# A fused retention and mixture kernel: all TensorE products but the scores in the 128x64 split, decay every second chunk, one written order with written ring places

## The chip, the cores and the metric

The kernel runs on one core of a Trainium2 chip. The metric is the device time of one execution in microseconds (us). A core has five engines with queues of their own: TensorE (PE; its weight loads are listed as PEld), VectorE (DVE), ScalarE (ACT), GpSimd (POOL) and SyncE (SP), which here only issues DMAs. An engine takes its instructions in the order in which the program issues them. Matrix products are written to PSUM, a second on-chip memory, from which DVE or ACT must copy them.

## The reference

Inputs are q, k and v of shape 8 x 8 x 576 x 64 (batch, heads, tokens, head size), w_in (512 x 1024), w_out (1024 x 512) and g_ln (1024), all float32. First comes retention, attention with a fixed decay for each head in place of a softmax, then a two-layer block over 4608 tokens of width 512:

```python
scores = q @ k.transpose(0, 1, 3, 2) / 8
gamma = 1 - 2.0 ** (-5 - arange(8))
Dmat = where(rel >= 0, gamma[:, None, None] ** rel, 0)
attn = (scores * Dmat) @ v
x = attn.transpose(0, 2, 1, 3).reshape(4608, 512)
h = x @ w_in
solu = h * softmax(h)
ln = (solu - mean(solu)) / sqrt(var(solu) + 1e-6) * g_ln
out = ln @ w_out
```

Here rel is the query's position less the key's.

## The kernel before

**Chunks.** The 576 tokens of a batch element are cut into four chunks of 128 tokens (c = 0 to 3) and one of 64 (c = 4). The 64-token chunks of two elements are put together, so there are 36 chunks of 128 rows; n counts them, in groups of nine: two elements in turn for c = 0 to 3, then their common c = 4. Retention is computed chunk by chunk: inside a chunk as masked scores, and from the chunks before through a state (64 x 64 for each head) that is decayed and added to.

**Steps.** The work of a chunk is a set of small functions, the steps, each named by two letters and issued for a chunk by a token such as `tq:8` or `ex:5:a`, whose last letter names the engine (a ACT, v DVE, g POOL). In the order of the data:

- `ld` loads q, k and v (768 KB, SP queue). `cq`, `ck`, `cv` turn them into float16, q and v times a decay table (L205 to L224).
- `tq` transposes q and k on PE (L226), `eq` copies both out of PSUM. From chunk 12 on `kd` transposes k by DMA instead (L237), `tr` transposes only q on PE (L250) and `er` copies it. Chunks with c = 4 keep the first way.
- `sc` makes the scores: eight matmuls with 64 rows and 128 columns of weights, two at a time in the two row halves of the array (L283). `mk` masks them on DVE (L296).
- `kv` makes this chunk's addition to the state, eight matmuls with 64 columns of weights (L306). `ad` adds it to the decayed state, on DVE (L320; the sum is the tile t). `dk` makes from t the float16 state for the next chunk's query (L334), and `d3` the decayed float32 state for the next `ad` (L346), both on POOL. `d3` runs for c = 0 to 2.
- `av` multiplies the masked scores with v (eight matmuls with 64 columns of weights, L358); `fs` adds query times state to the same PSUM bank (L373; nothing for c = 0). `ex` copies the sum to xT.
- `m1` makes h in eight 512-column matmuls (L405; `mr` does the same in parts for the first two chunks, L393). `mx` takes the row maximum on DVE, `xp` exp on ACT, `so` the product u on DVE. In the first five chunks (PLAIN) `ce` subtracts the mean; for later chunks the mean is taken out of w_out once instead (`mm`, `mc`, `ws`).
- `sq` squares and sums on ACT; `rt` turns the sums into the row factor rs by three tiny POOL instructions (w, w, rs; L470). `tu` transposes u on PE in eight matmuls (lp, L491) and `eu` copies lp to uT; for seven late chunks `du` transposes u by DMA. `m2` makes the output in eight 512-column matmuls (L508), `st` scales it by rs and stores it.
- `li`, `lo` load the weights; `wi`, `wo` convert them. The last chunk is done in halves by steps that begin with h.

**Order.** Nothing is scheduled by a compiler: tokens are issued in written order, and so each engine's queue is filled. START (L26) is the written begin, LOOP (L43) a fixed pattern issued for 21 chunks, and END (L47) the written end. In LOOP the PE steps stand in the order tr, tu, m1, kv, av, sc, fs, m2.

**Places.** PSUM has eight banks of 2 KB for each partition. h takes two of two (tag h); the other four are given out by the digits in BANKS (L63), one for each tile in the order of issue. A tile that takes a bank waits until the reader of the tile before it in that bank is done. SBUF tiles rotate through rings of a fixed number of buffers (`bufs`).

**Shapes of the array.** A row of the profile such as `128*64 128x128` says that the weights have 128 rows and 64 columns, and that 128 columns are streamed. Before, `kv` and `av` are 128\*64 (each pair of matmuls fills the left and the right half of the array's columns), `sc` is 64\*128, and all others are 128\*128.

Of the kernel before, what the change touches and what calls it, by code (L numbers as in the profile page):

```python
# [13 lines left out]
P = 128  # L14
# [4 lines left out]


PLAIN = 5
FIRST = 7
STEP = 1
STOP = 28
BY_DMA = 12
START = """  # L26
ld:0 ld:1 c1:0 ck:0:g cq:0:v cv:0:v li:3 gt:0 c2:0 tq:0 cq:1:g cv:1:v ld:2 kv:0 ck:1:v tq:1 ad:0
eq:1:a d3:0 cq:2:v cv:2:g li:2 li:0 eq:0:a kv:1 wi:3:1:a sc:1 li:1 mk:1 dk:0 sc:0 ck:2:a ld:4
av:1 wi:3:0:a wi:2:1:g fs:1 tq:2 ld:3 mk:0 ad:1 av:0 ex:1:a wi:0:0:g eq:2:a fs:0 wi:1:1:a kv:2
mr:1:3 ad:2 d3:1 wi:1:0:g wi:2:0:v cq:4:g wi:0:1:v d3:2 sc:2 mr:1:0 ex:0:v ld:5 mr:1:2 ld:6  # L30
mr:1:1 mr:0:0 mr:0:2 mk:2 ck:4:g mx:1 xp:1 mr:0:1 mr:0:3 av:2 dk:1 mx:0 tq:4 eq:4:a so:1 cv:4:g
ce:1 wu:0:4 fs:2 lo:1 lo:2 cq:3:v sc:4 ex:2:a ck:3:g cv:3:g tu:1 xp:0 mk:4 m1:2 sq:1 tq:3 eu:1:a
dk:2 kv:4 eq:3:a ck:5:a kv:3 av:4 cq:5:g so:0 fs:4 ad:3 d3:3 sc:3 mx:2 dk:3 cq:6:g ex:4:a mk:3
ad:4 tq:5 cv:5:g xp:2 eq:5:a m1:4 lo:0 lo:3 sc:5 d3:4 so:2 cv:6:g mk:5 dk:4 kv:5 av:3 ck:6:a
fs:3 tq:6 d3:6 wo:4:g av:5 ex:3:a ld:7 eq:6:a wo:1:g mx:4 ad:5 wo:7:g kv:6 xp:4 m1:3 fs:5 ce:0
ce:2 wo:2:a ex:5:a tu:0 tu:2 sc:6 wo:5:a m1:5 ld:8 ad:6 so:4 wo:3:a eu:2:v mk:6 rt:1 wo:6:v
wo:0:a sq:0 d3:5 av:6 sq:2 mx:5 fs:6 ck:7:g mm:0 m2:1 cq:7:g ld:9 mx:3 eu:0:a rt:2 mc:0:v m2:0
ce:4 cq:8:v ws:3:v rt:0 xp:3 tu:4 ex:6:a ws:7:v ld:10 ws:4:v ck:8:g dk:5 st:1 xp:5 tq:7 sq:4
so:3 eu:4:v ld:11 eq:7:a m2:2 st:0 so:5 tq:8 ce:3 eq:8:a m1:6 ws:1:v ws:0:v cv:7:g sc:7 ws:2:g
tu:3 st:2 rt:4 ws:5:v ld:12 m2:4 mk:7 sc:8 sq:3 eu:3:a cq:9:g mx:6 mk:8 m2:3 st:4 dk:6 rt:3  # L40
cq:10:g kv:7 ck:9:a ws:6:v xp:6 cv:9:v ad:7 cv:8:v st:3 av:7 fs:7 ex:7:a ck:10:a ck:11:a
"""
LOOP = """  # L43
tr:2 so:-1 tu:-2 ld:6 er:2:v m1:0 dk:0 kv:1 eu:-2:a kd:4 ad:1 cv:3:g av:1 mx:0 sc:2 sq:-2 fs:1
ex:1:a rt:-2 cq:4:g xp:0 m2:-2 d3:0 ck:5:g st:-2 mk:2
"""
END = """  # L47
d3:-7 tr:-5 kd:-3 cq:-3:g kv:-6 av:-6 er:-5:v ld:-1 ad:-6 tr:-4 fs:-6 ex:-6:a dk:-7 sq:-9
so:-8 sc:-5 m1:-7 cv:-4:g er:-4:v mk:-5 tr:-3 kd:0 kv:-5 ck:-2:g av:-5 sq:-8 fs:-5 tu:-8 mx:-7
ad:-5 rt:-9 cv:-3:g dk:-5 er:-3:a tu:-9 kd:-2 m1:-6 xp:-7 sc:-4 kv:-4 cq:-2:v eu:-9:v so:-7  # L50
ex:-5:a m1:-5 sc:-3 mk:-4 rt:-8 du:-7 d3:-6 ld:0 mx:-6 eu:-8:a d3:-5 mk:-3 ad:-4 ck:-1:a dk:-6
m2:-9 av:-4 mx:-5 xp:-6 kv:-3 av:-3 d3:-4 cv:-1:g st:-9 d3:-1 ad:-3 kd:-1 cv:-2:g d3:-2 cq:0:g
fs:-4 fs:-3 so:-6 tr:-2 er:-2:v ex:-4:a xp:-5 m2:-8 sq:-6 dk:-4 sc:-2 mk:-2 ck:0:g m1:-4 so:-5
kv:-2 kv:-1 du:-5 ex:-3:a av:-2 sq:-7 st:-8 mx:-4 sq:-5 xp:-4 fs:-2 m1:-3 cq:-1:v cv:0:g kq:-1
rt:-5 dk:-3 ex:-2:a d3:-3 ad:-2 du:-6 tr:0 so:-4 er:0:a m2:-7 sc:0 m1:-2 ad:-1 mk:0 mx:-3
sc:-1 rt:-6 mk:-1 mx:-2 m2:-5 sq:-4 du:-4 kv:0 rt:-7 rt:-4 av:-1 av:0 fs:-1 dk:-1 m2:-6 st:-7
# [37 lines left out]
def kernel(  # L94
# [683 lines left out]
```

## Time and profile before

| | |
|---|---|
| median of 3 runs | 219.55 us (218.33 to 220.63) |
| the profiled execution | 218.18 us, its span 216.5 us (first to last instruction) |
| PE | 197.4 us busy (91%), 1989 matmuls; 1989 weight loads |
| DVE | 180.8 us (84%), 289 instructions |
| ACT | 167.1 us (77%), 279 |
| POOL | 173.6 us (80%), 275 |
| DMA | 47.04 MB, mean 217 GB/s |
| granted TensorE clock | 1.00 |

Busy time is the union of an engine's records. Matmuls are pipelined: a row "0.61 ... x8" is the time from the first start to the last end, and the next row may start before that end, so the pace is read from differences of starts. In a waits view a line says which engine's instruction, by line number, waited for which other, and then the total in us, the number of waits and the longest. "issue" is time in which the engine waited for nothing that the profile shows.

### The profile page before, as it was taken

How to read it: one execution, taken by the hardware profiler on the slowest of the kernel's cores; microseconds unless marked ns; L12 is line 12 of the kernel's file. 1: busy time of each engine (PE TensorE's matmuls, PEld its weight loads, DVE VectorE, ACT ScalarE, POOL GpSimd, SP SyncE). 2: the span in 40 equal slices, each digit the busy share in tenths (PEclk: the TensorE clock that was granted, in tenths of full speed). 3: DMA queues.
4: the chain of work that ended last, by engine and by line, in shares of the span. 5: the costliest groups of instructions: out<-in, count | busy, mean ns of one | idle time of the engine just before them, and what ended most of it. 6: DMA issues, size and time to landing. Idle time of an engine off the chain costs nothing.

```text
span 216.5 us, 5376 instructions
## 1 busy us (share of the span) xinstructions
PE 197.4 (91%) x1989; PEld 110.8 (51%) x1989; DVE 180.8 (84%) x289; ACT 167.1 (77%) x279; POOL 173.6 (80%) x275
## 2 busy tenths in 40 slices
PE   0379889896999999999999999999999999999993
PEld 0254456453455555555555555555555565545451
DVE  1378899999997998888888898888888999889840
ACT  2073988966897888888888788888888794986991
POOL 3348889997367899999997899999997899977340
PEclk9999999999999999999999999999999999999999
DMA  5999999998986899799999998899999999674845
GB/s 137 289 317 287 228 280 358 193 245 224 270 228 168 219 183 201 177 225 258 243 223 232 255 208 186 186 247 248 214 227 213 253 181 190 145 172 100 195 109 182
DMA packets 112250, 47.04 MB, mean 217 GB/s; under 512 B 96984, under 2 KB 106208, under 8 KB 112224
## 3 DMA queue, kind: packets, MB, share of 16 engines
q1 hardware_dynamic: 111904, 46.55, 92.7%
q8 instruction: 15, 0.25, 0.5%
q10 hardware_dynamic: 320, 0.16, 0.3%
q14 instruction: 11, 0.09, 0.2%
HBM read 32.54 MB, written 9.44 MB: 194 GB/s over the span
## 4 chain that ended last, share of the span: by engine, by line
PE 78%; DVE 13%; DMA 2%; issue 2%; SPq 2%; ACT 1%; DVEq 0%; ACTq 0%
PE o L515 26%; PE h L412 23%; PE sc L290 5%; PE lp L495 5%; PE x L365 4%; PE x L380 3%; PE kp L314 3%; DVE nm L422 3%; DVE ret L303 2%; DMA vf<-in_v_dram 2%; PE tp L232 2%; PE tr L256 2%; PE h L400 2%; DVE u L437 2%; DVE q L210 1%
## 5 line engine op out<-in xcount | busy, mean ns | idle before, releaser
L412 PE MATMUL h<-w_in,xT 128*128 128x512 f16 x264 | 62.4, 379 | 0.5 <-DVE u L437 0.5
L515 PE MATMUL o<-w_c,uT 128*128 128x512 f16 x240 | 56.5, 379 | 0.6 <-DVE t L327 0.4
L428 ACT ACTIVATE e<-h,nm 128x1024 f32<-128x1024 f32 x35 | 39.0, 1116 | 14.0 <-DVE nm L422 14.0
L303 DVE TENSOR_TENSOR ret<-sc,tris 128x512 f16<-128x512 f32 x72 | 46.1, 682 | 1.3 <-PE sc L290 1.2
L437 DVE SCALAR_TENSOR_TENSOR u<-h,e 128x1024 f16<-128x1024 f32 x35 | 42.7, 1220 | 2.7 <-ACT e L428 1.4
L422 DVE TENSOR_REDUCE nm<-h 128x1 f32<-128x1024 f32 x35 | 42.5, 1216 | 2.0 <-PE h L412 1.5
L515 PEld LDWEIGHTS <-uT 128*128 128x128 f16 x280 | 26.2, 98 | 27.1 <-issue 0.4
L412 PEld LDWEIGHTS <-xT 128*128 128x128 f16 x264 | 24.2, 98 | 24.4 <-issue 0.5
L341 POOL TENSOR_TENSOR s<-t,small 128x512 f16<-128x512 f32 x32 | 34.2, 1070 | 2.6 <-DVE t L329 2.6
L199 POOL TENSOR_TENSOR v<-vf,small 128x512 f16<-128x512 f32 x32 | 33.6, 1051 | 3.0 <-DMA vf<-in_v_dram 3.0
L465 ACT ACTIVATE sq<-u,su 128x1024 bf16<-128x1024 f16 x30 | 34.8, 1159 | 0.1
L210 POOL TENSOR_TENSOR q<-qf,small 128x512 f16<-128x512 f32 x30 | 31.3, 1044 | 1.8 <-DMA qf<-in_q_dram 1.8
L171 ACT CAST xT<-x 128x512 f16<-128x512 f32 x34 | 19.9, 585 | 11.1 <-PE x L380 10.6
L523 ACT ACTIVATE o_sb<-o,rs 128x512 f32<-128x512 f32 x35 | 23.9, 685 | 4.1 <-POOL rs L487 1.6
L171 ACT COPY uT<-lp 128x1024 f16<-128x1024 f16 x25 | 25.3, 1012 | 0.3 <-PE lp L495 0.2
L487 POOL TENSOR_TENSOR rs<-w,mhalf 128x1 f32<-128x1 f32 x36 | 19.8, 551 | 3.0
L483 POOL TENSOR_SCALAR w<-ss,w 128x1 f32<-128x1 f32 x31 | 8.9, 287 | 15.9 <-ACT sq L465 13.9
L171 POOL CAST k<-kf 128x512 f16<-128x512 f32 x28 | 17.1, 611 | 3.0 <-DMA kf<-in_k_dram 3.0
L171 ACT COPY qkT<-tp 128x512 f16<-128x512 f16 x20 | 10.7, 594 | 10.9 <-PE tp L232 10.9
L495 PE MATMUL lp<-ident,u 128*128 128x128 f16 x224 | 17.0, 219 | 1.3 <-DVE u L453 1.3
L353 POOL TENSOR_TENSOR s<-t,small 128x256 f32<-128x256 f32 x24 | 14.9, 622 | 3.4 <-DVE t L327 2.5
L290 PE MATMUL sc<-qkT 64*128 64x128 f16 x288 | 15.2, 225 | 2.0 <-ACT qkT L171 1.2
(89 smaller groups left out, 262.5 us busy)
## 6 DMA issues: line engine op xcount, KB each, us to landing
qf<-in_q_dram SPq DMA_DIRECT2D x32, 256.0 KB, 4.0
kf<-in_k_dram SPq DMA_DIRECT2D x32, 256.0 KB, 4.4
vf<-in_v_dram SPq DMA_DIRECT2D x32, 256.0 KB, 4.7
out_dram<-o_sb SPq DMA_DIRECT2D x32, 256.0 KB, 2.6
w_in<-in_moe_w_in_dram SPq DMA_DIRECT2D x4, 512.0 KB, 6.1
w_out<-in_moe_w_out_dram SPq DMA_DIRECT2D x4, 512.0 KB, 6.7
qf<-in_q_dram SPq DMA_DIRECT2D x8, 128.0 KB, 3.2
kf<-in_k_dram SPq DMA_DIRECT2D x8, 128.0 KB, 3.8
```

The lines of the kernel that those rows point to most:

```text
L171: (engine.copy if engine is nc.scalar else engine.tensor_copy)(out=out, in_=in_)
L199: engine.tensor_tensor(out=dst, in0=T.pop((key, n)), in1=table.unsqueeze(2).to_broadcast([P, H, D]), op=ALU.mult,)
L210: ENG[e].tensor_tensor(out=dst.rearrange("p (a h) d -> p h a d", h=2), in0=T.pop(("qf", n)).rearrange("p (h a) d -> p h a d", h=2), in1=ta ...
L303: nc.vector.tensor_tensor(out=r, in0=s, in1=m, op=ALU.mult)
L341: nc.gpsimd.tensor_tensor(out=s16, in0=t.unsqueeze(2).to_broadcast([P, 4, 2, D]), in1=gd.unsqueeze(3).to_broadcast([P, 4, 2, D]), op=ALU.mult,
L412: nc.tensor.matmul(out=h[:, i * 512 : (i + 1) * 512], lhsT=xT[:, d], rhs=w_in16[:, d, i * 512 : (i + 1) * 512], start=d == 0, stop=d == 3,)
L422: nc.vector.tensor_reduce(out=nm, in_=T["h", n], axis=AX.X, op=ALU.max, negate=True)
L428: nc.scalar.activation(out=e, in_=T["h", n], func=ACT.Exp, bias=T.pop(("nm", n)), accum_out=s)
L437: nc.vector.scalar_tensor_tensor(out=u, in0=T.pop(("h", n)), scalar=-1.0, in1=T.pop(("e", n)), op0=ALU.mult, op1=ALU.mult, accum_out=su,)
L465: nc.scalar.activation(out=s, in_=T.pop(("v", n)), func=ACT.Square, scale=-float(DFF), bias=T.pop(("su", n)), accum_out=ss,)
L495: nc.tensor.transpose(out=lp[:, c], in_=u[:, c * P : (c + 1) * P], identity=ident)
L515: nc.tensor.matmul(out=o, lhsT=uT[:, c], rhs=w[:, c], start=c == 0, stop=c == NF - 1)
```

## The change

- **Split.** Two helpers, `turn` and `product`, replace each transpose and each 128-column matmul by two, one for each half of the weight columns, which write the two halves of the output's partitions. Only `sc` and one tiny transpose at the start keep their shape.
- **Decay.** A pair of chunks (c = 0 and 1, 2 and 3) shares one frame: the tables of the odd and even chunk differ (`frame`), `ad` of an odd chunk adds to t of the even one directly, and `d3` runs only for c = 1, with the factor of 256 tokens. `dk` stays in each chunk with a factor that depends on c. The constant table grows from 52 to 100 columns.
- **Order.** START, LOOP and END are replaced by one written list, ORDER, of all steps of all chunks. In it some copies and conversions change engine. `rt` is cut into `ra` (two instructions, POOL or DVE) and `rp` (one, POOL).
- **Places.** Each ring tile's buffer is written down in SLOTS, in the order of allocation. The sizes of the rings stay, but t has 4 buffers instead of 2, the decayed float32 state 2 instead of 4, the four s16 buffers are shared by all batch elements, and tiny tiles have 40 buffers each instead of 6.

The diff, cut to its core:

```diff
+ORDER = """
+ld:0 c1:0 gt:0 c2:0 cv:0:g ck:0:a ld:1 ck:1:g cq:1:g li:0 wi:0:0:g cq:0:v tq:0 eq:0:va sc:0 kv:0
+ad:0 tq:1 eq:1:va ld:2 sc:1 li:3 dk:0 mk:0 av:0 li:2 cq:2:g mk:1 ex:0:v ck:2:a tq:2 eq:2:a cv:1:g
+sc:2 mk:2 wi:3:0:a kv:1 av:1 wi:3:1:g wi:0:1:a mr:0:0 li:1 ex:1:a cv:2:g wi:2:0:g wi:1:1:g kv:2
+ad:2 d3:2 av:2 fs:2 ld:4 cq:4:g mr:1:3 cv:4:g mr:1:0 ad:1 dk:2 wi:1:0:v ld:3 cq:3:g wi:2:1:a
+mr:1:2 ex:2:a mr:1:1 mx:1 ck:4:a mr:0:2 mr:0:1 mr:0:3 mx:0 xp:1 dk:1 ld:5 cq:5:g tq:4 eq:4:a
+cv:3:g so:1 kv:4 sc:4 xp:0 ld:6 lo:1 lo:3 ad:4 ck:5:g ce:1 m1:2 ck:3:a tq:3 mk:4 sq:1 av:4 fs:4
+so:0 ra:1:g dk:4 wu:0:4 mx:2 tu:1 eq:3:a ex:4:a ck:6:g ce:0 sc:3 mk:3 rp:1 xp:2 so:2 tq:5 m1:4
+cq:6:g cv:5:g kv:3 eu:1:a ad:3 av:3 fs:3 eq:5:a dk:3 d3:3 tu:0 cv:6:g wo:7:g mx:4 ce:2 ex:3:a sc:5
...
+rp:5 rp:3 ld:12 cv:12:g m1:7 cv:11:g st:4 so:6 tr:11 er:11:a ws:1:v tr:10 ex:8:a mx:7 ld:13 xp:7
+m2:3 st:3 ld:14 ck:12:g av:9 ex:9:a ws:4:v sq:6 ra:6:g ws:6:v er:10:v m2:5 st:5 so:7 sq:7 sc:10
+mk:10 kv:9 ad:9 cq:12:g m1:8 dk:9 tu:6 cv:10:v kd:12 tu:7 ck:13:a kd:13 ld:16 sc:11 eu:6:a mx:8
+xp:8 mk:11 m1:9 eu:7:a kv:12 rp:6 cv:13:g av:10 m2:6 kv:11 so:8 sq:8 st:6 ex:10:v kv:10 cq:14:g
+mx:9 xp:9 m1:10 tr:12 ad:10 dk:10 cq:13:g ad:11 ld:15 ck:14:a ad:12 er:12:a tr:14 ra:7:v av:11
+so:9 kd:14 er:14:a ra:8:g fs:11 ex:11:v dk:11 sq:9 ra:9:g ck:16:a m2:7 kd:16 ld:19 sc:12 mx:10
+xp:10 mk:12 tu:8 m1:11 rp:7 eu:8:v rp:8 dk:12 st:7 av:12 so:10 fs:12 ex:12:a cv:14:g mx:11 tr:13
+er:13:a tu:9 eu:9:a m2:8 cq:15:v sc:13 ld:18 ck:15:a kd:15 cv:16:v kv:14 mk:13 m1:12 st:8 d3:12
+ad:14 sc:14 xp:11 so:11 mk:14 cv:15:g rp:9 ld:17 tu:10 m2:9 cq:16:g kv:16 sq:10 ra:10:g mx:12
...
+mk:35 du:31 av:34 so:33 du:30 so:32 fs:34 ex:34:a cv:35:g du:33 dk:34 m2:30 av:35 dk:33 fs:35
+ex:35:v du:32 m1:34 mx:34 sq:33 sq:32 ra:33:g rp:33 hm:35:0 hm:35:1 st:29 hx:35:0 hx:35:1 st:30
+m2:33 xp:34 hp:35:1 so:34 rp:31 du:34 m2:32 hp:35:0 ra:32:g st:33 ho:35:1 ho:35:0 hc:35 sq:34
+ht:35:1 he:35:1:v ra:34:g ht:35:0 rp:34 he:35:0:v rp:32 hq:35:0:v hq:35:1:a ra:35:v m2:31 h2:35:0
+rp:35 st:31 st:32 m2:34 hw:35:0:a st:34 h2:35:1 hw:35:1:v
 """
...
+RINGS = dict(
+    qf=7, kf=6, vf=7, q16=5, k16=6, v16=5, qkT=4, ret0=4, ret1=4, xT=4, t=4, s16=4, s32=2, h=2,
+    e=3, u=5, uT=5, o_sb=4,
+)
+SLOTS = """
+qf 012345601234560123450621534261504261
+kf 012345012345012345012340152401532410
...
+h 010010101010101010101010101010101011
...
+t 01230120312031023021320310231032
+s16 01230120310231021302130213023101
...
+    head, at = 2 * (p[:, None] % 4) + j // 4, 4 * (p[:, None] // 4) + j % 4
+    by_token = [g[None, :] ** e[:, None] for e in (p - 128, p, p % 64)]
+    by_four = [g[head] ** e for e in (at - 128, at, at % 64)]
+    gq = [x / 8.0 for x in by_four + by_token]
+    gk = [1.0 / x for x in by_token]
...
     gs = np.zeros((P, 4))
-    gd = np.zeros((P, 4, 2))
+    gd = np.zeros((3, P, 4, 2))
     for e in range(2):
         for hp in range(4):
-            gs[e * 64 : e * 64 + 64, hp] = g[2 * hp + e] ** 128.0
-        gd[e * 64 : e * 64 + 64, :, e] = gs[e * 64 : e * 64 + 64]
-    small = np.concatenate([gq, gk, gqt, gkt, gs, gd.reshape(P, 8), gqm], axis=1).astype(np.float32)
+            w = slice(64 * e, 64 * e + 64)
+            gs[w, hp] = g[2 * hp + e] ** 256.0
+            for i, power in enumerate((0.0, 256.0, 128.0)):
+                gd[i, w, hp, e] = g[2 * hp + e] ** power
...
-    tiny = ctx.enter_context(tc.tile_pool(name="tiny", bufs=6))
+    tiny = ctx.enter_context(tc.tile_pool(name="tiny", bufs=40))
...
+    def frame(n):
+
+        return 2 if chunks[n][1] == 4 else chunks[n][1] % 2
...
+    def ring(pool, shape, dtype, name):
+
+        at = int(next(slots[name]))
+        assert at < RINGS[name]
+        return pool.tile(shape, dtype, tag=f"{name}_{at}", name=name, bufs=1)
...
+    HALF = (slice(0, 64), slice(64, P))
+
+    def turn(out, in_):
+
+        for w in HALF:
+            nc.tensor.transpose(out=out[w], in_=in_[:, w], identity=ident)
+
+    def product(out, lhsT, rhs, start, stop):
+
+        for w in HALF:
+            nc.tensor.matmul(
+                out=out[w], lhsT=lhsT[:, w], rhs=rhs, start=start, stop=stop,
+                skip_group_check=True,
+            )
+
...
-        dst = half.tile([P, H, D], F16, name="q16", bufs=5)
+            return scaled(n, "qf", "q16", gq[frame(n)], ENG[e])
+        table = gq4[frame(n)]
+        dst = ring(half, [P, H, D], F16, "q16")
         ENG[e].tensor_tensor(
             out=dst.rearrange("p (a h) d -> p h a d", h=2),
...
         T["t", n] = t
+        if c % 2 == 0:
+            T["s32", b, c + 1] = t
...
-            in1=gd.unsqueeze(3).to_broadcast([P, 4, 2, D]), op=ALU.mult,
+            in1=gd[(0, 1, 0, 2)[c]].unsqueeze(3).to_broadcast([P, 4, 2, D]), op=ALU.mult,
...
     def d3(n):
 
-        if chunks[n][1] >= 3:
+        if chunks[n][1] != 1:
             return
         (b,), c = chunks[n]
-        s32 = stp.tile([P, 4, D], FP, tag=f"s32_{b % 2}", name="s32")
+        s32 = ring(stp, [P, 4, D], FP, "s32")
...
     def fs(n):
 
         bs, c = chunks[n]
-        qkT = T.pop(("qkT", n))
-        s16 = [T.pop(("s16", b, c)) for b in bs] if c > 0 else []
+        if c == 0:
+            return
+        qkT = T["qkT", n]
+        s16 = [T.pop(("s16", b, c)) for b in bs]
...
-    def rt(n):
+    def ra(n, e="g"):
 
         w1 = tiny.tile([P, 1], FP, name="w1")
         w2 = tiny.tile([P, 1], FP, name="w2")
-        rs = tiny.tile([P, 1], FP, name="rs")
         s = T.pop(("s", n))
-        nc.gpsimd.tensor_scalar(
+        ENG[e].tensor_scalar(
             out=w1, in0=s, scalar1=s, scalar2=1e-6 * DFF, op0=ALU.mult, op1=ALU.mult
         )
         if n < PLAIN:
-            nc.gpsimd.tensor_tensor(out=w2, in0=w1, in1=T.pop(("ss", n)), op=ALU.add)
+            ENG[e].tensor_tensor(out=w2, in0=w1, in1=T.pop(("ss", n)), op=ALU.add)
         else:
-            nc.gpsimd.tensor_scalar(
+            ENG[e].tensor_scalar(
                 out=w2, in0=T.pop(("ss", n)), scalar1=1.0 / DFF**2, scalar2=w1, op0=ALU.mult,
                 op1=ALU.add,
             )
-        nc.gpsimd.tensor_tensor(out=rs, in0=w2, in1=mhalf, op=ALU.pow)
+        T["w2", n] = w2
+
+    def rp(n):
+
+        rs = tiny.tile([P, 1], FP, name="rs")
+        nc.gpsimd.tensor_tensor(out=rs, in0=T.pop(("w2", n)), in1=mhalf, op=ALU.pow)
         T["rs", n] = rs
...
-            nc.tensor.transpose(out=lp[:, c], in_=u[:, c * P : (c + 1) * P], identity=ident)
+            turn(lp[:, c], u[:, c * P : (c + 1) * P])
...
         for c in range(NF):
-            nc.tensor.matmul(
-                out=o, lhsT=uT[:, c], rhs=w[:, c], start=c == 0, stop=c == NF - 1
-            )
+            product(o, uT[:, c], w[:, c], c == 0, c == NF - 1)
...
     with tc.manual_schedule():
-        run(START, 0)
-        for i in range(FIRST, STOP - STEP + 1, STEP):
-            run(LOOP, i)
-        run(END, NCH - 1)
+        run(ORDER, 0)
```

More of the change, by code (lines that the diff above doesn't have):

```diff
@@ L618, in h2 @@
         for c in range(NF):
-            nc.tensor.matmul(
-                out=o, lhsT=T["huT", n, c // 4][:, c % 4], rhs=T["w_c"][:, c, w], start=c == 0,
-                stop=c == NF - 1,
-            )
+            product(o, T["huT", n, c // 4][:, c % 4], T["w_c"][:, c, w], c == 0, c == NF - 1)
         T["ho", n, i] = o
@@ L720, in mm @@
         for c in range(NF):
-            nc.tensor.matmul(
-                out=T["mean"], lhsT=ones, rhs=w_out16[:, c], start=c == 0, stop=c == NF - 1
-            )
+            product(T["mean"], ones, w_out16[:, c], c == 0, c == NF - 1)
     def mc(_, e):
```

235 lines of the change are left out of this document (118 added, 117 removed).

## The prediction

> **What bounds the kernel now.** I read the chain of work that ended last first, then busy time by stage, then TensorE's (PE's) timeline in one steady stretch. The chain, by engine:
>
> ```profile
> PE 78%; DVE 13%; DMA 2%; issue 2%; SPq 2%; ACT 1%; DVEq 0%; ACTq 0%
> ```
>
> By stage (columns: span, then busy time and count of PE, PEld, DVE, ACT, POOL; granted clock; DMA share; GB/s):
>
> ```profile
> 0.00:20.00 20.00, 10.12 (x95) 6.08 (x96) 9.36 (x20) 7.17 (x12) 8.87 (x22) 1.00 1.00 260
> 20.00:52.00 32.00, 27.32 (x275) 15.64 (x274) 31.29 (x48) 25.49 (x45) 29.93 (x40) 1.00 1.03 253
> 60.00:160.00 100.00, 99.51 (x1056) 56.52 (x1054) 88.19 (x136) 84.72 (x134) 92.33 (x142) 1.00 0.95 217
> ```
>
> VectorE (DVE) sets the pace from 20 to 52 us (31.3 of 32 busy), PE after that. The handover is in PE's timeline: m2:2, then tq:8, which waited for DVE's eu:4.
>
> ```profile
> 48.30 1.89 PE L515 MATMUL o<-w_out,uT 128*128 128x512 f16 x8
> 52.05 0.38 PE L232 MATMUL tp<-ident,q 128*128 128x128 f16 x4 [1.86 <-DVE uT L171]
> ```
>
> In the steady part PE never idles, but not all of its time streams columns. Read the differences of starts (first column):
>
> ```profile
> 100.38 1.89 PE L515 MATMUL o<-w_c,uT 128*128 128x512 f16 x8
> 102.10 0.39 PE L232 MATMUL tp<-ident,q 128*128 128x128 f16 x4
> 102.33 0.39 PE L232 MATMUL tp<-ident,k 128*128 128x128 f16 x4
> 102.55 0.61 PE L495 MATMUL lp<-ident,u 128*128 128x128 f16 x8
> 103.00 1.89 PE L412 MATMUL h<-w_in,xT 128*128 128x512 f16 x8
> 104.82 0.32 PE L314 MATMUL kp<-v,k 128*64 128x64 f16 x8
> 104.96 0.39 PE L365 MATMUL x<-ret,v 128*64 128x128 f16 x8
> 105.29 0.40 PE L290 MATMUL sc<-qkT 64*128 64x128 f16 x8
> 105.62 0.40 PE L380 MATMUL x<-qkT,s 128*128 128x128 f16 x4
> 105.85 1.89 PE L515 MATMUL o<-w_c,uT 128*128 128x512 f16 x8
> ```
>
> Eight 512-column matmuls followed by the same shape take 1.72 us (o to tp: 215 ns each); followed by 128*64 they take 1.82 (h to kp). lp takes 0.45 for eight (56 ns each). sc (64*128) to L380 (128*128) takes 0.33 where eight in pairs need 0.23. So each change of the array's split costs about 0.10; over the single records of the trace the cheap ones are 92 to 96 ns, median about 94.
>
> **The account before.** PE streams 580 x 0.2155 (512 columns) + 16 x 0.109 + 560 x 0.056, 32 of them at half length + 144 pairs of sc and 144 of x x 0.056 + 32 kp steps x 0.14 = 178 us. In the written order the split changes 120 times: 11.3 us. The last matmul ends near 212.5, so 212.5 - 178 - 11.3 = 23 us are waits, nearly all before 52. Output after it: 4.0.
>
> **The split.** What streams is unchanged if halves run side by side. x does: 8 half matmuls (4 pairs) of 128 columns add no more than 4 transposes of full width (0.33 - 0.10 = 0.23 against 102.33 - 102.10 = 0.23). So 512 columns in two halves cost 0.2155; if the second half's start, 3 to 4 ns later in the records, added to each pair: 580 x 4 ns = +2.3, the upper end. I take 0, as x is the nearest row. Weight loads of 64 columns take 113 ns (L365) against 98 for 128, and stay hidden in the x row. [...] Counting the new order, all but sc share a split, sc steps stand alone or in twos: 65 changes instead of 120. Those before the handover are covered by DVE's queue (cover gone, another 0.8): after tq:8 there were 92, and after the new order's matching place (tu:5) 46 are left: 46 x 0.094 = **-4.3**.
>
> **The start.** Order and DVE's own issue intervals (ret 0.60, nm 1.13, u 1.14, t 0.34, uT and xT 0.60): up to eu:4 DVE had 35.1 us of work and PE 28.6 ahead of tq:8, lead 6.5; DVE ran 16.8 late (51.9 - 35.1), of which about 10 are first loads. In the new order the worst DVE-to-PE lead is mk:8 to tu:5, 37.4 - 31.7 = 5.7. With the same lateness: **-0.8**; if the first chunks start earlier or later by what the first loads vary here (vf waits 2.3 us at DVE), -2 to +2. The first h still waits for w_in, whose four loads (li) are again among the first seven loading steps of SP.
>
> **Decay every second chunk.** d3 falls from 24 to 8: 16 x 0.622 = 10.0 us off POOL. POOL also loses 8 of 36 ra (8 x 0.57 = 4.6) and 8 ck (4.9), gains 3 cq, 2 cv, 1 wi (5.8): 173.6 to about 160. PE waits for POOL only through DVE's t:
>
> ```profile
> DVE t L329 <- POOL s L341: 5.1, 9, 0.6
> ```
>
> All PE waits after 52 beyond the split changes are about 3.2 us, so this relief is worth 0 to -3.2. DVE: 11 more uT (7.5), 18 fewer qkT copies (12.1), 5 xT (3.4), ra (2.3), the rest -3.8: 180.8 to 178. ACT: 11 uT fewer (11.1), 18 qkT more (10.7), ck and xT even: unchanged. At 178/36 = 4.94 streaming plus 1.3 changes x 0.094 = 5.06 us a chunk, DVE at 88.19/100 x 5.24 = 4.6 still fits.
>
> **The written order and places.** They issue nothing. The larger constant table (52 to 100 columns) is hidden by qf, for which DVE waits 3.36 us; uncovered, its whole landing, 1.6. On PE the steps between a producer and its consumer mostly grow (medians, us of PE work: m1 to tu 7.7 to 9.4, tu to m2 2.5 to 4.2, tr to sc 2.5 to 4.7), but are uneven: fs to m1 was never under 2.39 and is now under 1.6 three times. xT takes 0.59, with up to 1.1 of ACT ahead of it, so such places cost 0 to 0.7 each. On SP, loads wait behind kd, which waits for ck (19.5 us in ten waits before); those waits move with it. The 8 ra on DVE can hold its queue for sq, with mk and mx behind (POOL waited for sq 6.4 us in 8 waits from 60 to 170): 0 to 1.2 each, most of it in DVE's slack. New waits: 0 to +4. Against POOL's relief I net both to 0, keeping -3.2 and +4.
>
> **PE's instructions** go from 3978 to about 6290. The trace's steady row has 2110 in 100 us, 95 ns a matmul with its load; the new order asks 88 matmuls in 5.06 us, 57 ns. The dense stretch from 182.73 to 184.13 has 36 in 1.40, 39 ns, but the queue may have run ahead there. At 39 it costs nothing, at 95 88 x 95 = 8.4 us a chunk, +100 in all. I take 0, as the dense row is what a full queue looks like. Fetching them grows from 0.25 MB in 15 transfers to about 0.40, of 47 MB; PE waits for none of the 15.
>
> **Sum:** 218.2 (span 216.5 + 1.7 around it) - 4.3 - 0.8 + 0 = 213.1 on the profiled execution's scale. That execution lies 1.4 under the median of 219.55, so 214.5 on the median's; I say 214.0.
>
> **Rivals.**
> - PE's instruction supply becomes the bound: slower. Place: every packed chunk. It decides above 57 ns a matmul, and 5 ns above that costs 88 x 5 = 0.44 us in some 30 chunks, 13 us: 227. For: no long stretch shows better than 95. Against: the 39 ns stretch, and eight kp in 0.14. Chance 0.15. [...]
> - The gain is spent on waits: 217 to 221.5. A place: cv:12 in POOL's queue, reached after 49.9 us of POOL work plus 7 to 10 of first waits (before, 11 by 20 us). It needs 13 chunks (0.786 MB each) and 4.2 MB of weights: 14.4 MB at 256 GB/s is 56 us, so a margin of 1 to 3. If missed, ra and rp behind it, then st and the banks, are late. 0.17.
> - More is gained: POOL's relief counts fully, 209 to 211. 0.12.
> - Halves do not run side by side: +580 x 0.216, 339. The x row speaks against it. 0.03.
> - The forecast, 211 to 217: 0.53.
>
> **Numbers.** About 1% is what a measurement can tell. Faster by more: 0.53 + 0.12 + 0.03 of the second rival = 0.68; within: 0.14; slower: 0.18. The range, 208.5 to 221, leaves out the supply case, the 339 and little else.
>
> **What would show it.** Right: o, h and lp rows as 128*64 with twice the count, still 1.72 from o to the next step of the same split; L314 no longer behind "issue"; PE packed from about 52; the last matmul near 208. Wrong: pairs of transposes above 56 ns or 512-column pairs above 216 (supply or no overlap); PE waits of over 3 us after 60; POOL waiting for vf near 57; handover later than 53.

## The result, and the profile after

The changed kernel takes 231.91 us (median of 4, 230.85 to 234.56) where the kernel before takes 218.94 (218.15 to 220.63) beside it: 1.0565 times as long, 95% interval 1.0472 to 1.0659. Forecast were 214.0, range 208.5 to 221. The profiled execution took 232.25, its span is 230.4. Some executions of each kernel are slower than the rest with nothing changed; ratios and intervals, and all medians from here on, are over the others (231.56 us for the changed kernel). So 13 us were lost where 4 to 5 were to be won. Three views answer to those shown of the kernel before.

The chain of work that ended last, by engine:

```profile
PE 36%; DVE 25%; DMA 13%; SPq 7%; ACT 6%; POOL 5%; issue 5%; POOLq 0%; DVEq 0%; ACTq 0%
```

PE's share fell from 78% to 36%. DMA and SyncE's queue (SPq), together 4% before, have 20%.

The stages (span, busy time of PE, PEld, DVE, ACT, POOL with counts, granted clock, DMA share, GB/s), and below them three stretches of 10 us:

```profile
0.00:20.00 20.00, 8.97 (x135) 6.42 (x137) 7.93 (x17) 6.91 (x11) 11.22 (x24) 1.00 0.96 259
20.00:52.00 32.00, 28.61 (x488) 19.12 (x486) 30.66 (x52) 26.89 (x48) 28.52 (x37) 1.00 0.99 252
60.00:160.00 100.00, 89.68 (x1453) 56.91 (x1450) 80.49 (x129) 73.81 (x127) 73.44 (x110) 0.97 0.94 213
...
100.00:110.00 10.00, 7.92 (x130) 5.74 (x132) 5.16 (x9) 6.36 (x12) 7.62 (x12) 0.83 0.99 239
150.00:160.00 10.00, 8.62 (x128) 5.28 (x130) 8.27 (x13) 4.14 (x9) 7.59 (x10) 0.83 0.96 222
180.00:190.00 10.00, 5.72 (x94) 4.04 (x90) 4.38 (x8) 4.80 (x9) 7.27 (x9) 0.85 0.69 183
```

Up to 52 us PE was busy as long as before (37.6 us against 37.4). From 60 to 160 all four engines do less, and the DMA engines, though 94% busy, carry 213 GB/s instead of 217.

PE's timeline in a stretch without waits shows that the split itself did as forecast:

```profile
118.09 1.92 PE L252 MATMUL h<-w_in,xT 128*64 128x512 f16 x16
119.84 0.39 PE L446 MATMUL x<-ret,v 128*64 128x128 f16 x8
120.06 0.39 PE L247 MATMUL tr<-ident,q 128*64 128x128 f16 x8
120.29 0.61 PE L247 MATMUL lp<-ident,u 128*64 128x128 f16 x16
120.73 0.29 PE L393 MATMUL kp<-v,k 128*64 128x64 f16 x8
120.86 1.90 PE L252 MATMUL h<-w_in,xT 128*64 128x512 f16 x16
122.59 0.61 PE L247 MATMUL lp<-ident,u 128*64 128x128 f16 x16
```

Sixteen half matmuls of 512 columns take 1.73 us (120.86 to 122.59; before, eight whole ones took 1.72), sixteen of 128 columns 0.44 (0.45 before), and nothing is added where kp begins or ends. What was lost stands in the same timeline behind the square brackets (idle before, and its releaser). These are PE's waits after 90 us that took over 0.9 us:

```profile
94.73 0.40 PE L369 MATMUL sc<-qkT 64*128 64x128 f16 x8 [1.35 <-DMA qkT<-k]
102.08 0.64 PE L252 MATMUL x<-qkT,s 128*64 128x128 f16 x8 [2.71 <-POOL s L422]
117.76 0.40 PE L369 MATMUL sc<-qkT 64*128 64x128 f16 x8 [0.92 <-DMA qkT<-k]
137.01 0.32 PE L393 MATMUL kp<-v,k 128*64 128x64 f16 x8 [1.21 <-ACT o_sb L603]
151.36 0.82 PE L369 MATMUL sc<-qkT 64*128 64x128 f16 x16 [1.94 <-DMA qkT<-k]
187.35 0.64 PE L446 MATMUL x<-ret,v 128*64 128x128 f16 x8 [4.28 <-POOL v L282]
```

All of PE's waits after 52 us make 14.5 us; before they made 2.5, of which 1.86 stand at the handover itself. Of the six shown, three are for transposed k, and two for POOL, which itself waited for loads. Its queue ahead of the wait at 102.08, whose releaser is the s that ends there:

```profile
92.36 0.61 POOL L239 CAST k<-kf 128x512 f16<-128x512 f32 x1 [3.79 <-DMA kf<-in_k_dram]
94.32 1.04 POOL L282 TENSOR_TENSOR v<-vf,small 128x512 f16<-128x512 f32 x1 [1.35 <-DMA vf<-in_v_dram]
...
98.89 0.61 POOL L239 CAST k<-kf 128x512 f16<-128x512 f32 x1 [1.78 <-DMA kf<-in_k_dram]
99.46 0.55 POOL L569 TENSOR_TENSOR rs<-w,mhalf 128x1 f32<-128x1 f32 x1
99.98 1.04 POOL L293 TENSOR_TENSOR q<-qf,small 128x512 f16<-128x512 f32 x1
100.98 1.04 POOL L422 TENSOR_TENSOR s<-t,small 128x512 f16<-128x512 f32 x1
```

SyncE sent the load that the cast at 98.89 waited for only at 95.06, after 2.62 us for a transpose of k and 1.90 for two stores:

```profile
89.03 2.62 SPq L322 DMA_TRANSPOSE qkT<-k  x1
91.75 1.90 SPq L608 DMA_DIRECT2D out_dram<-o_sb  x2
93.74 1.27 SPq L268 DMA_DIRECT2D qf<-in_q_dram  x2
95.06 1.31 SPq L275 DMA_DIRECT2D kf<-in_k_dram  x2
```

Over the whole page POOL's casts of k waited 11.3 us for loads, before 3.0.

### The profile page after: what moved, and what is told of

It reads as the page before. It is cut to its first block, busy times and chain, and to the rows that moved or that the text cites. A ratio compares the mean times of both kernels' runs of the same rounds, so it can differ in the third digit from the quotient of the medians.

```text
span 230.4 us, 7656 instructions
## 1 busy us (share of the span) xinstructions
PE 197.2 (86%) x3145; PEld 125.3 (54%) x3145; DVE 179.6 (78%) x300; ACT 165.5 (72%) x286; POOL 161.3 (70%) x241
## 2 busy tenths in 40 slices
DMA packets 112258, 47.21 MB, mean 205 GB/s; under 512 B 96984, under 2 KB 106208, under 8 KB 112224
## 4 chain that ended last, share of the span: by engine, by line
PE 36%; DVE 25%; DMA 13%; SPq 7%; ACT 6%; POOL 5%; issue 5%; POOLq 0%; DVEq 0%; ACTq 0%
PE o L252 12%; PE h L252 12%; DMA kf<-in_k_dram 6%; DVE ret L382 5%; DVE nm L500 5%; DVE u L515 5%; DMA qkT<-k 3%; SPq L275 3%; SPq L268 3%; DMA w_in<-in_moe_w_in_dram 3%; ACT e L506 2%; PE x L446 2%; PE sc L369 2%; PE lp L247 2%; DVE u L531 2%
## 5 line engine op out<-in xcount | busy, mean ns | idle before, releaser
L252 PE MATMUL h<-w_in,xT 128*64 128x512 f16 x560 | 68.2, 387 | 0.0
L252 PE MATMUL o<-w_c,uT 128*64 128x512 f16 x480 | 57.9, 385 | 0.3 <-DMA uT<-u 0.2
L252 PEld LDWEIGHTS <-uT 128*64 128x64 f16 x560 | 31.2, 112 | 24.6 <-issue 2.3
L252 PEld LDWEIGHTS <-xT 128*64 128x64 f16 x576 | 31.1, 111 | 23.5 <-issue 0.7
L239 ACT CAST xT<-x 128x512 f16<-128x512 f32 x29 | 17.2, 592 | 7.5 <-PE x L252 6.5
L239 POOL CAST k<-kf 128x512 f16<-128x512 f32 x20 | 12.2, 610 | 14.4 <-DMA kf<-in_k_dram 11.3
L446 PE MATMUL x<-ret,v 128*64 128x128 f16 x288 | 15.7, 235 | 5.0 <-POOL v L282 4.3
L369 PEld LDWEIGHTS <-qkT 64*128 64x128 f16 x288 | 8.7, 97 | 20.5 <-DMA qkT<-k 7.2
L247 PE MATMUL lp<-ident,u 128*64 128x128 f16 x448 | 17.3, 223 | 1.4 <-DVE ret L382 1.0
L247 PEld LDWEIGHTS <-u 128*64 128x64 f16 x448 | 14.8, 112 | 3.3 <-issue 1.5
```

The source lines that it names most:

```text
L239: (engine.copy if engine is nc.scalar else engine.tensor_copy)(out=out, in_=in_)
L247: nc.tensor.transpose(out=out[w], in_=in_[:, w], identity=ident)
L252: nc.tensor.matmul(out=out[w], lhsT=lhsT[:, w], rhs=rhs, start=start, stop=stop, skip_group_check=True,)
L369: nc.tensor.matmul(out=s[e][:, hp], lhsT=qkT[dd, 1, hp], rhs=qkT[dd, 0, hp], start=True, stop=True,)
```

## The experiments

Ratios are to the kernel before, run beside it (217.8 to 218.5 us); square brackets hold the 95% interval. "Old order" is START, LOOP and END of the kernel before.

**One part at a time.** The first four kernels were to say which part loses. e1 is the kernel before with the two helpers of the change put in:

```diff
-            nc.tensor.matmul(out=o, lhsT=uT[:, c], rhs=w[:, c], start=c == 0, stop=c == NF - 1)
+            product(o, uT[:, c], w[:, c], c == 0, c == NF - 1)
```

> The kernel before with the two split helpers alone; order, places and decay as before. Theory W (the split is free and saves its 94 ns for each change of the array's split; the loss of the changed kernel is waits that its written order makes, above all late loads): split changes fall from 120 to 71, after the handover from 92 to 58, so 34 x 0.094 = 3.2 us less, some of it lost to POOL, which was nearly level with PE: 215 to 218 against 219. Rival S (the split itself costs, by the clock of 0.978 or by the doubled instructions): 224 or more, with a clock under 1.

Measured: 221.63 us, 1.0208 [1.0116, 1.0301]. Slower by 1 to 3%, but not by the split: in the trace the pairs take 216 and 56 ns, and from 60 to 118 us no wait of TensorE is new. Then it waits for transposed k:

```profile
123.77 0.40 PE L301 MATMUL sc<-qkT 64*128 64x128 f16 x8 [0.45 <-DMA qkT<-k]
141.64 0.40 PE L301 MATMUL sc<-qkT 64*128 64x128 f16 x8 [2.36 <-DMA qkT<-k]
```

e4 is the changed kernel with the old order written out, `rt` as `ra` and `rp` on POOL, the old BANKS, and rings that turn by themselves:

```diff
-        at = int(next(slots[name]))
-        return pool.tile(shape, dtype, tag=f"{name}_{at}", name=name, bufs=1)
+        return pool.tile(shape, dtype, tag=name, name=name, bufs=RINGS[name])
```

> Split, shared decay frames and the rt cut into ra and rp (both on POOL), but the order and the bank digits of the kernel before and rings that rotate by themselves. Theory W: as the split alone and up to 2 us less, since 16 d3 (10 us of POOL) are gone: 213 to 217. Rival D (the shared frame lengthens the chain from state to state, or POOL's freed time only moves the wait): 1 us or more above the split alone. Rival S: 224 or more.

Measured: 219.36, 1.0079 [1.0033, 1.0126]: the decay, which relieves POOL of 10 us (174.1 busy in e1, 164.1 here), takes 2.3 of e1's 3.6 us back, together with the ring sizes that came with it. e2 is the changed kernel with one full-width instruction for each pair:

```diff
-        for w in HALF:
-            nc.tensor.matmul(out=out[w], lhsT=lhsT[:, w], rhs=rhs, start=start, stop=stop, ...)
+        nc.tensor.matmul(out=out, lhsT=lhsT, rhs=rhs, start=start, stop=stop, ...)
```

> The changed kernel with its two helpers issuing one full-width instruction again: the new order and places without the split; 161 split changes instead of 65. Theory W: PE gets 96 x 0.094 = 9 us more to do, about half of it hidden in the waits: 233 to 241. Rival S (the split costs): 231 or less.

Measured: 231.74, 1.0644 [1.0539, 1.0750], the same as the changed kernel. So the new order makes the loss (with its places and its choice of engines, which no run takes apart), and the 96 changes of shape that the split saves in it are worth nothing there. e3 writes the loads from chunk 7 on as early in the new order as their ring places allow:

```diff
-... ck:13:a kd:13 ld:16 sc:11 ...   (each ld where the change has it)
+... each ld:n right behind the last cast that read its place
```

> The changed kernel with one thing moved: each load from chunk 7 on stands in the written order at the first place where its ring places are free, 5 to 20 us of PE work earlier; nothing else is reordered. Theory W: the waits of POOL for kf and vf and of PE behind them go, 214 to 222. Rival O (the uneven order of the compute steps makes the waits, loads are only where they show): 228 to 232.

Measured: 232.60, 1.0683 [1.0598, 1.0769]. The waits moved and did not shrink: PE's waits for transposed k, written behind those loads, grew from 4.9 to 10.0 us after 52. Late loads alone are not the cause.

**Lighter transfers.** One thing was common to e1, e3, e4 and the changed kernel: waits for transfers that were late, while the packets of e1 and e4 took 94% of their spans on the DMA engines. Each load of k or v is 1,024 packets of 256 bytes. The next kernels load the same bytes in 128 packets of 2 KB, and so other elements:

```diff
-    out=dst[pp], in_=src[b, :, s0 : s0 + m, :].rearrange("h p d -> p h d")
+    out=dst[pp].rearrange("p h d -> p (h d)"),
+    in_=src[b].rearrange("h s d -> (h s d)")[s0 * H * D : (s0 + m) * H * D]
+        .rearrange("(p x) -> p x", x=H * D),
```

> The kernel before with the split alone, and with k and v loaded as contiguous rows of 2 KB: the same bytes into the same tiles by the same instructions, but other elements of k and v than the reference's, 128 packets for a tile in place of 1,024. With the true loads the split alone took 222.4 us where before took 218.1. Theory N (the DMA engines' packet time, 93% of the span there, lies just under TensorE's and comes through as late transposes of k): the 256-byte packets of k and v cost about 2.6 us of each chunk's 5.1 us of DMA time, and go to about half, so the DMA share falls from 94% to about 75%, the waits of the scores for the transposed k are gone, and the time is 209 to 214. Theory S (the split itself costs or the old order has no use for it, whatever the transfers): 219 to 224.

> The kernel before, unchanged but for k and v loaded as contiguous rows of 2 KB (other elements of k and v than the reference's). The control to the split with the same loads. Theory N: TensorE alone bounds, 213 to 218, and the split with light loads is 3 to 5 us below this one, as the 46 changes fewer say. Theory S: 215 to 219, and the split with light loads lies at or above this one.

> The changed kernel with k and v loaded as contiguous rows of 2 KB (other elements of k and v than the reference's). Theory N (the new order loses 14 us through transfers that are late): the waits of POOL for the loads and of the scores for the transposed k shrink, and the time falls from 231.9 to 210 to 217. Rival O (the new compute order makes TensorE wait for POOL, ACT and DVE whatever the transfers do): 224 to 231.

Measured: e5 218.48, 1.0032 [0.9994, 1.0071]; e6 217.94, 1.0038 [0.9998, 1.0077]; e7 214.60, 0.9881 [0.9788, 0.9974]. The kernel before does not care about the packets (e6), the split alone gains 3.2 us by lighter ones (e5), the changed kernel 17.0 (e7). Rival O, that the new compute order makes the waits by itself, falls. e7's stretch from 60 to 160, and the packets and main queue of the changed kernel and of e7:

```profile
60.00:160.00 100.00, 98.26 (x1670) 62.57 (x1668) 92.07 (x148) 85.08 (x144) 82.68 (x120) 1.00 0.97 242
```

```profile
DMA packets 112258, 47.21 MB, mean 205 GB/s; under 512 B 96984, under 2 KB 106208, under 8 KB 112224
q1 hardware_dynamic: 111904, 46.55, 86.9%
```

```profile
DMA packets 47746, 47.21 MB, mean 222 GB/s; under 512 B 23256, under 2 KB 32480, under 8 KB 47712
q1 hardware_dynamic: 47392, 46.55, 83.6%
```

The same 47.21 MB in 64,512 fewer packets: PE is busy 98.3 of 100 us and the DMA engines deliver 242 GB/s, since the kernel now asks for it. The packet time falls from 0.869 x 230.4 = 200 us to 0.836 x 212.5 = 178; in the kernel before, with its steadier demand, from 0.927 x 216.5 = 201 to 167.

That e5 lies at e6's level was not expected by theory N (it should have been 3 to 5 us lower). e11 adds the decay to e5, e10 takes the split out of e7:

> The old order with split and decay, and k and v loaded as contiguous rows of 2 KB (other elements of k and v than the reference's). With the same loads the kernel before takes 217.9 and the split alone 218.5, with POOL busy 96% of the stretch from 80 to 160 us in both. If POOL was what kept the split from paying in the old order (theory P), the decay's relief of POOL lets the 46 fewer changes through: 212.5 to 215. If the order itself keeps it (theory O2: start and drain of the old order are what is lost): 216.5 to 219.

> The changed order, ring places and decay with one full-width instruction in place of each pair (161 changes of shape on TensorE in place of 65), and with k and v loaded as contiguous rows of 2 KB (other elements of k and v than the reference's). With the true loads the split made no difference in this order (231.7 without, 231.9 with). Theory N: with transfers out of the way TensorE bounds again and the 96 changes of 94 ns are paid: the changed kernel with the same loads (214.6) plus up to 9.0, that is 220 to 224. Rival (the split is worth nothing in this order, other waits set the time): 213 to 217.

Measured: e11 216.78, 0.9933 [0.9905, 0.9961]; e10 219.28, 1.0067 [1.0019, 1.0115]. With light packets the split is worth 219.28 - 214.60 = 4.7 us in the new order, 96 changes fewer, of which 9.0 were possible: PE's waits after 52 are 0.7 us in e10 and 4.1 in e7. The old order gains 217.94 - 216.78 = 1.2 by split and decay together, where its 34 fewer changes after 52 (92 to 58) would be worth 3.2. Where the other 2 us stay the runs do not show.

**Which queue issues.** e8 issues the stores from ACT's queue in place of SyncE's; e9 does the same with the transposes of k, and e12 with those of e4:

```diff
-            nc.sync.dma_start(out=out[b * S + s0 : b * S + s0 + m, :], in_=o_sb[pp])
+            nc.scalar.dma_start(out=out[b * S + s0 : b * S + s0 + m, :], in_=o_sb[pp])
```

> The changed kernel with its stores issued from ScalarE's queue, right behind the instruction that makes the tile, in place of SyncE's: the result is the reference's. In the changed kernel SyncE's queue stands 16 us of its time in front of stores whose tile is not ready, with loads and transposes of k queued behind. Theory Q (this queueing on SyncE makes the transfers late): loads and transposes start earlier, 231.9 falls to 220 to 226. Theory N (packet time, not the queue): the DMA engines are as busy as before in total and the time stays at 228 to 232; ScalarE's added issues may cost 0 to 3 us.

> The changed kernel with the transposing transfers of k (kd) issued from ScalarE's queue, at the same places of the written order, in place of SyncE's: the result is the reference's. They then stand neither behind loads nor in front of them on SyncE. Theory Q (transfers are late because SyncE's queue is in order): 231.9 falls to 220 to 226. Theory N (the DMA engines are full for a packet stream that the order asks for faster than they carry it, whichever queue issues): 228 to 235, ScalarE now waiting for POOL's k16 at some of the 24 places.

> The old order with split and decay (219.6 against 218.1 for before), with the transposing transfers of k issued from ScalarE's queue: the result is the reference's. Its waits on TensorE after 120 us are for these transfers. Theory Q: they come earlier, 215 to 218, a version faster than both kernels. Theory N: they are late because the DMA engines are full and k16 comes late from POOL: 218 to 223, with ScalarE held where k16 is not ready.

Measured: e8 231.04, 1.0637 [1.0497, 1.0777]; e9 237.87, 1.0909 [1.0813, 1.1004]; e12 221.66, 1.0139 [1.0074, 1.0203]. None gains. That another queue is no way out is shown; that SyncE's queue costs nothing is not, for ACT pays in its place: in e12's waits view ACT's sq alone stands 13.0 us in 13 waits from 52 to 200 us, put down to POOL's s, where in the whole page of the kernel before sq waits 0.1 us.

**The floor of the transfers.** Why does the new order suffer so much more from the same transfers? e13 (old order, split and decay) and e14 (the changed kernel) leave out half of the second product, 30 us of PE's work:

```diff
-        for c in range(NF):
-            product(o, uT[:, c], w[:, c], c == 0, c == NF - 1)
+        for c in range(0, NF, 2):
+            product(o, uT[:, c], w[:, c], c == 0, c == NF - 2)
```

> The old order with split and decay, with four of the eight pairs of the second product (o) left out, so that TensorE has about 30 us less to do and can't be the bound; all transfers are as they were. What remains is the floor that transfers, SyncE's queue and the other engines set. Theory N (the packets' time of about 200 us, plus a start and an end that don't fill the DMA engines): 207 to 216, against 219.6 whole. If the transfers had slack in the old order: 190 to 203.

> The changed kernel with four of the eight pairs of the second product (o) left out, all transfers as they were: the floor of the new order's transfers without TensorE as a bound. Theory C (capacity alone, the loss comes from TensorE and the transfers taking turns): the same floor as the old order's, 207 to 216. Theory U (the written order holds the transfers up itself: loads, stores and transposes stand behind work that is not ready, with leads from 0 to 42 us of TensorE's work in place of an even 11 to 21): 222 to 231, hardly less than the whole kernel's 231.9.

Measured: e13 216.02, 0.9893 [0.9843, 0.9943]; e14 229.10, 1.0474 [1.0441, 1.0506]. PE, relieved of 30 us, gives back 3.3 in the old order and 2.5 in the new. e13's PE and its main DMA queue:

```profile
PE 173.0 (80%) x2865; PEld 114.1 (53%) x2865; DVE 178.8 (83%) x289; ACT 165.6 (77%) x279; POOL 164.8 (76%) x259
q1 hardware_dynamic: 111904, 46.55, 95.2%
```

PE is at 80%, the main queue's packets take 95% of the DMA engines' time: without PE as a bound the old order has a floor of 216, 2.5 us under the kernel before. That it is the transfers' floor is the likely reading, since the DMA share is 0.98 from 60 to 160 us and half of PE's 22.7 us of waits after 52 is for transposed k; no run takes SyncE's issuing or the other engines out of it. The new order's floor is 13 us higher with the same packets, so capacity alone (C) is not the cause; the order holds the transfers up.

**What holds them.** e15 writes each transpose of k in e4 one iteration later, e16 puts the stores and 11 transposes of the changed kernel later on SyncE's queue, so that what reaches its head is ready:

```diff
-eu:-2:a kd:4 ad:1
+eu:-2:a kd:3 ad:1
```

> The old order with split and decay, and each transposing transfer of k written one iteration later, still some 8 us of TensorE's work ahead of its scores: the result is the reference's. In the old order SyncE's queue stands about 28 us at these transfers because POOL's k16 is not ready, with the next loads behind them. Theory U (what stands at the head of SyncE's queue makes loads late): the next loads go out earlier, 215.5 to 218.5, a version below both kernels. Theory C (the DMA engines are simply full): 218.5 to 221.

> The changed kernel with its stores put on SyncE's queue some 2.6 us of TensorE's work later than their tiles are made, and 11 of the 24 transposes of k up to 4 us of it later than their k16, so that what comes to the head of the queue is ready more often; no engine's other work is moved and the result is the reference's. Theory U: loads behind them start earlier, 231.9 falls to 222 to 228. Theory C: 229 to 233.

Measured: e15 229.67, 1.0504 [1.0447, 1.0562]; e16 231.78, 1.0603 [1.0573, 1.0633]. Theory U as put there falls, and with it its premise, which came from the waits view. Chunk by chunk in e4's trace, the cast of k16 had ended 2.6 to 9.3 us before its transpose was issued, and in the changed kernel from 67 to 160 us every store's tile was done 0.9 to 15 us before its issue. SyncE was not held by tiles there, it was behind with issuing; the engine that the view names for such an issue is the one whose instruction happened to end last.

But e15 showed what does count. A transpose takes about 4 us from issue to landing (median 4.2 in the kernel before, 4.6 in e4, 3.8 in the changed kernel), and about 5 instead of 10 us of PE's work ahead of its scores cost the old order 10 us. So I looked at such leads in the written orders: us of PE's work between two tokens for chunks 12 to 33, each step at the pace of its starts (h and o 1.72, lp 0.45, sc 0.33, x and tr 0.23, kp 0.14), median and in brackets least and most. The expectations of e14 to e18 count the same leads by the steps' full records, which overlap, and so about a quarter longer.

```
                     old order              new order
load to cast of k     9.4 (7.6 to 9.6)       9.3 (2.9 to 34.2)
load to cast of v    16.9 (13.3 to 17.2)    18.7 (0.0 to 54.2)
transpose to scores  10.2 (8.1 to 10.5)     10.2 (4.2 to 15.7)
```

The medians are nearly equal, but the old order's leads are even, and the new one's go down to 2.9 and 4.2. e17 gives the changed kernel more even leads: for chunks 12 to 35 loads, casts and transposes are written so that no load stands less than 8.1 us ahead of its cast of k and no transpose less than 9.0 ahead of its scores. That takes one more place for k16 and two for qkT:

```diff
-    qf=7, kf=6, vf=7, q16=5, k16=6, v16=5, qkT=4, ...
+    qf=7, kf=6, vf=7, q16=5, k16=7, v16=5, qkT=6, ...
-... tu:5 av:7 st:2 fs:7 ex:7:a dk:7 ws:2:g tr:9 cq:11:v er:9:a ...
+... tu:5 av:7 st:2 fs:7 ex:7:a dk:7 ws:2:g tr:9 ld:13 cq:11:v er:9:a ...
```

> The changed kernel with nothing moved on TensorE, DVE's and ACT's own work in its order, but for chunks 12 to 35 the loads, the casts of k, q and v and the transposes of k written so that each stands at least as far ahead of its reader as in the old order (load 11 us or more of TensorE's work ahead of the cast, transposes 12 us or more ahead of the scores, where the change has as little as 4 and 5; places newly given, k16 in 7 and qkT in 6): the result is the reference's. Theory U2 (the short leads are what makes the same transfers cost 12 to 17 us): 231.9 falls to 216 to 223. Theory U3 (the leads don't matter, the lateness comes from how the compute order and the transfers chain up): 228 to 234.

Measured: 223.36, 1.0227 [1.0165, 1.0288]: 8.2 of the 13 us come back, by the leads and the three places together. The loads' leads alone do not do it: e3 had raised their least to 12.0 us, with the transposes still at 4.2, and won nothing. PE's waits for transposed k are gone; the three longest that are left after 52:

```profile
PE sc L369 <- DVE t L408: 3.1, 1, 3.1
PE kp L393 <- ACT o_sb L603: 3.1, 1, 3.1
PE x L446 <- ACT o_sb L603: 0.9, 1, 0.9
```

The first two come from loads as well. A cast of k on DVE waited 3.97 us, with t behind it, and one on POOL 7.39, with rs and so ACT's o_sb behind it:

```profile
148.62 0.60 DVE L239 CAST k<-kf 128x512 f16<-128x512 f32 x1 [3.97 <-DMA kf<-in_k_dram]
```

```profile
116.16 0.61 POOL L239 CAST k<-kf 128x512 f16<-128x512 f32 x1 [7.39 <-DMA kf<-in_k_dram]
```

e18 gives the old order with split and decay still longer leads, loads one iteration earlier and one place more in each load ring:

```diff
-ld:6 er:2:v
+ld:7 er:2:v
```

> The old order with split and decay, with each load from chunk 13 on written one iteration (some 5 us of TensorE's work) further ahead and one place more in each of the three load rings: the result is the reference's, the transfers' bytes, packets and issues are the same. If what is left there is short leads (theory U2): the casts of k and with them the transposes come in time, and the time falls from 219.6 to the floor with light packets, 216 to 217.5, the fastest correct version. If it is capacity (theory C): 218.5 to 221, since the DMA engines have no more to give in this stretch.

Measured: 220.11, 1.0102 [1.0046, 1.0158], no better than e4 (1.0079). So longer leads of the loads (14.2 us in place of 9.4) do not help in the old order, which fits capacity (C) there. No version with the reference's own data came out below the kernel before.

## Why the prediction was wrong, point by point

- **What bounds the kernel.** Right for PE, but half of it. The chain gave DMA 2%, and the stage rows in the prediction showed DMA shares of 1.00, 1.03 and 0.95, which its text did not use. e13 says what they meant: without PE a floor of 216, most likely the transfers', lies right under PE's 218. A chain names the bound that is on top, not the one beneath it.
- **The split.** Right: taken at 0, measured at 0 (sixteen half matmuls of 512 columns in 1.73 us, sixteen of 128 in 0.44).
- **Changes of shape.** Size and count right (into sc 96 ns, out of it 90; 65 changes). But -4.3 could be had only where PE bounds: 4.7 in the new order with light packets, 0 with the true ones.
- **The start.** The way is right: after 52 the first wait of PE is 0.47 us, at 61.04, and the columns streamed by 52 us make 1.7 us more than before, where 0.8 were said.
- **Decay every second chunk.** POOL 161.3 us (said about 160), DVE 179.6 (178), ACT 165.5 (unchanged said). The relief of 0 to -3.2 was 2.3 in the old order with true loads, 1.7 with light ones. That it fell in the range is in part luck: the waits that it took away are e1's (7.0 us after 52, in e4 4.8); the kernel before has only 0.6 after its handover.
- **The written order and places: the step that failed.** It priced "New waits: 0 to +4" from the steps on PE, where "the steps between a producer and its consumer mostly grow", and let loads behind the transposes off with "those waits move with it". Measured: waits of 14.5 us after 52 in place of 2.5, and 4.5 us more from the clock (below). The lead of the transfers, which fell to 3 and 4 us, was not looked at. And the "19.5 us in ten waits" of kd for ck were no such waits: in the kernel before, each of the 21 transposes was issued 0.95 to 6.5 us after its own cast had ended. The long issues came from a SyncE that was already late, with DMA engines 95% busy; so the sum had no term for a queue that runs late with its own issuing (a transpose took 1.94 us of SyncE there, 1.22 with light loads).
- **PE's instructions.** Right at 0: sixteen half matmuls in 0.44 us are 28 ns each, e7 keeps up 1,670 matmuls in 100 us, 60 ns each with the long ones among them, and fetching grew to 0.39 MB in 24 transfers. So the rival of instruction supply, by the trace's 95 ns a matmul, falls.
- **The sum.** 213.1 on the profiled execution's scale, 214.0 on the median's; with lighter transfers e7 took 214.26 and 214.60. That is near, but not a proof of each term: against e6, its own control, e7 wins 3.3 us where the terms said 5.1, with 3.5 us more of waits.
- **The rivals.** "The gain is spent on waits" had the mechanism, loads late at POOL with rs and the rest of its queue behind, at 0.17, but one place (cv:12 near 57, where nothing came late) and an end of 221.5. The lateness came at five and more places from 94 us on, so this rival's size was wrong by 10 us.
- **What stays open:** the 5 us between e17 and the kernel before; how much of e17's gain is the transposes' leads and how much the three places; why the old order with light packets keeps only 1.2 of 3.2 us; and whether the packets' time on the DMA engines or SyncE's issuing is the tighter limit, since light loads relieve both.

## What to carry to other kernels

Before pricing a faster engine, read the DMA share beside it: here 93% of the span meant a second bound close under the first, and taking work off the first engine (half of a product, in one run) shows how close it lies. When an order is written by hand or by a planner, look at the shortest lead of each kind of transfer and not at the median: here it had to cover the landing time (3.8 to 4.6 us for a transpose) and the lateness of the queue that issues it. In this kernel larger packets in place of those of 256 bytes were worth 17 us in the new order and nothing in the kernel before. And before a wait on a DMA queue is put down to a tile, look up in the trace when that tile was done.

## What the runs showed of the hardware

**A wait can cost more than itself.** After the wait of 2.71 us at 102.08, TensorE ran at half speed for about 3 us:

```profile
102.08 0.64 PE L252 MATMUL x<-qkT,s 128*64 128x128 f16 x8 [2.71 <-POOL s L422]
102.51 0.63 PE L247 MATMUL tp<-ident,q 128*64 128x128 f16 x8
102.93 0.63 PE L247 MATMUL tp<-ident,k 128*64 128x128 f16 x8
103.36 0.63 PE L446 MATMUL x<-ret,v 128*64 128x128 f16 x8
103.79 0.63 PE L252 MATMUL x<-qkT,s 128*64 128x128 f16 x8
104.21 2.29 PE L252 MATMUL o<-w_c,uT 128*64 128x512 f16 x16
106.33 0.61 PE L247 MATMUL tr<-ident,q 128*64 128x128 f16 x16
```

A step of eight takes 0.43 us, where at 120.06 it took 0.23, and o 2.12 instead of 1.73: 1.4 us more. The same follows the waits of 1.94 (h 2.78, o 2.38: 1.7 more) and 4.28 us (1.35), not those of 1.35 and less; together 4.5 of the 13 us lost, and the reason for the granted clock of 0.83 to 0.85 in the three stretches. Not every wait does it: one of 1.86 in the kernel before, of 2.36 in e1 and of 3.06 in e17 (ending at 149.70) left the clock at 1.00, while another of 3.06 in e17 (ending at 118.80) was followed by 6.8 us at half speed (clock 0.70, 0.50 and 0.95 in the three windows of 4 us from 116 us on).

In the changed kernel the trace's records of the granted clock show half speed from 101.59, 152.79 and 186.92 us, for 3.41 us each: the first and the third began 0.49 and 0.43 us before their waits ended, the second 1.43 us after. The starts are 51.20 and 34.13 us apart, 15 and 10 times 3.413. Cut the trace along them into pieces of that length: after the first 12.8 us there are three pieces at full speed in which PE was idle for over half, and they are the three just ahead of the starts, with 65%, 58% and 100%. In the other pieces at full speed up to 227.9 us PE was idle for 49% or less, and none of them was followed by half speed. (In the first 12.8 us pieces with up to 71% left the clock at 1.00; why, the trace does not say.) So in this trace a piece need not be idle throughout, and waits of 1.94 and 2.71 us were enough. For the spared wait of e17 (146.64 to 149.70) an estimate: its stretch at half speed began near 117.6 us, by the clock of 0.70 from 116 to 120, and nine lengths of 3.413 us later is 148.3, within the wait, with about 1.7 us on one side and 1.4 on the other. What sets the clock no run shows.

**In the kernel before, SyncE's issues took longer with the packets of 256 bytes.** A transpose of k of the kernel before, and one of e7:

```profile
106.51 2.67 SPq L241 DMA_TRANSPOSE qkT<-k  x1
```

```profile
101.42 1.23 SPq L330 DMA_TRANSPOSE qkT<-k  x1
```

Over 60 to 160 us their medians are 1.94 in the kernel before and 1.22 in e6, its twin with light packets. A DMA share near 1 alone does not do it: in e7 it is 0.97 in that stretch, and the nine transposes that stand singly in SyncE's timeline have a median of 1.23. The length is not a wait for the tile: the k16 of the first one was done 2.58 us before that issue began, and where SyncE does wait, the wait stands ahead of the record (a store of the changed kernel starts at 187.03 after 2.5 us of waiting, 0.03 us behind the end of its o_sb). All of SyncE's issues from 60 to 160 us take 86.4 us in the kernel before, 67.3 in e6 and 91.0 in the changed kernel. So with the true loads the queue of the kernel before has 19 us more of issuing in these 100 us than e6's, and what stands behind it goes out later without waiting for any tile.
